# Weight pieces requested one ahead instead of up to four ahead, in an attention + two-MoE kernel

## The chip, the cores and the metric

The kernel runs on one core of a Trainium2 chip. The metric is the device time of one execution in microseconds (us). An execution uses TensorE (PE, and PEld for its weight loads), VectorE (DVE), ScalarE (ACT), GpSimd (POOL), SyncE (SP), which here does nothing but request DMAs, and 16 DMA engines that carry what SP and POOL request.

## What is computed

Three stages follow one another, all in float32:

```python
# 1: block-causal attention, 4 batches x 8 heads x 576 positions x 64
scores = scale * np.matmul(q, k.transpose(0, 1, 3, 2))
mask = block_i >= block_j                      # blocks of 64
attn = softmax(where(mask, scores, -1e9));  x = attn @ v      # as (2304, 512)
# 2: a gated feed-forward layer with d_ff = 1536
gate = 1.0 / (1.0 + np.exp(-(x @ w_gate)));  val = x @ w_val
x = (gate * val @ w_out).astype(np.float32)
# 3: top-1 routing of the 2304 tokens to 8 experts with 1024 hidden columns
out[mask] = gate_w[mask, None] * (np.maximum(xe @ w1[e], 0.0) @ w2[e])
```

The three matrices of stage 2 arrive as 8-byte floats. They have to be turned into pairs of 4-byte numbers (a high and a low part) on the core before TensorE can use them.

## The kernel before, in words

**Attention.** A *pair* is two heads of one batch; there are 16 pairs of five *items* (128 query rows each, the last 64). Pairs 0 to 3, the first batch, run alone ("quick" phase, the function `quick`, up to about 110 us); the other pairs are mixed with stage 2. For a pair `load(p)` requests nine DMAs on SP: keys (two, plus a tail and the tail of the queries into the same tile), queries (two) and values (three). The key tile `k` and the query tile `q` exist once, the value tile `v` twice. So a request for keys waits until the transposes of the keys before have read the tile (L216, the function `prep`), and one for values until the last product with the values of two pairs earlier (L382).

`quick(i)` emits the scores of item i+2 and the product with the values of item i. The load of pair p+1 is written at the end of `quick(i)` for item i = the first of pair p. The transposes of those keys stand in the very next `quick`, which is one item later. The transposed keys are copied by ACT (the tail of the queries, L221, first) and DVE (`kn`, L223), and the scores of the last item of a pair (L256) follow.

**Weights.** Stage 2's matrices are cut into 27 *pieces*, numbered p0, p1, ... here: p0 to p14 have 1024 columns (1 MB each as 8-byte numbers, two DMAs, L557), p15 to p26 have 256. The raw bytes of the large ones go into four tiles (`spare_90` to `spare_93` in the rows, p_n in number n mod 4; p12 to p14 take 91, 92 and 93 again), those of the small ones into three (`wtmp`). A piece is decoded in steps by ACT and DVE: ACT L569 is the first step and the first reader, DVE L574 the last reader of the raw bytes (it frees the tile), then L579, the cast L588 and the subtraction L590. The generator `weights()` emits these steps; `quick` pulls about two steps at each item, so a piece is begun about every second item, and `w_load` requests pieces from inside it. `w_load(NPI)` requests every piece whose tile is free by the order of the program, so up to four ahead.

**Queues.** SP takes its requests in the order in which the program wrote them, and a request that must wait for a tile holds all that come after it. The order on SP is therefore what decides whether keys come before or after weight bytes. PE, ACT, DVE and POOL have orders of their own, given by the program too.

**Stage 2.** Tokens go in units of 256. The attention output x is written to `x_d` by POOL (L393), and `load_x` (L623) reads the four tiles `xu` of a unit back on SP's queue. PE multiplies them with the decoded pieces (`gv`, L634 to L636), ACT and DVE make `g` (L655 to L659), and `acc` (L671) is the product with w_out.

Of the kernel before, what the change touches and what calls it, by code (L numbers as in the profile page):

```python
# [24 lines left out]
def attn_moe_moe_kernel(  # L25
# [473 lines left out]
    NBIG = NW - 3  # L499
    pieces = []  # L500
    for i in range(NW):
        f = i // 3 * 2 + (1 if i % 3 == 2 else 0)
        n = 1024 if i < NBIG else 256
# [11 lines left out]
    NPI = len(pieces)  # L515
# [14 lines left out]
    def before(n):  # L530

        if n >= NBIG:
            return three[n % 3], (n - 3 if n >= NBIG + 3 else -1)
        if n < NW - 6:
            return words[n % 4], n - 4
        return words[(n + 1) % 4], n - 3
# [13 lines left out]
    def w_load(n):  # L550
        while wload[0] < min(n, NPI) and before(wload[0])[1] <= wread[0]:
            dst = before(wload[0])[0]
            o = 0
            for src, r0, nk, c0, ncol in pieces[wload[0]][3]:
                w = nk * ncol * wn
                x = src.bitcast(I32)[r0:r0 + nk * P, c0 * wn:(c0 + ncol) * wn]
                nc.sync.dma_start(  # L557
                    out=dst[:, o:o + w].rearrange("p (k c) -> p k c", k=nk), in_=x.rearrange("(k p) c -> p k c", p=P)
                )
                o += w  # L560
            wload[0] += 1

    def w_round(n, stage):

        raw_ = w_raw(n)
        w0, w1 = raw_[:, :, 0], raw_[:, :, 1]
        b, r = w_buf(n), w_res(n)
        if stage == 0:
            nc.scalar.activation(out=r, in_=w0.bitcast(U32), func=AF.Copy, scale=2.0 ** -29)  # L569
            nc.vector.tensor_scalar(  # L570
                out=b, in0=w1, scalar1=3, scalar2=0x3FFFFFFF, op0=ALU.logical_shift_left, op1=ALU.bitwise_and
            )
        elif stage == 1:
            nc.vector.scalar_tensor_tensor(  # L574
                out=b, in0=w1, scalar=-0x40000000, in1=b, op0=ALU.bitwise_and, op1=ALU.bitwise_or
            )
            wread[0] = n
        else:
            nc.vector.tensor_tensor(out=b, in0=b, in1=r, op=ALU.add)  # L579

    def w_split(n, stage):
        i, c, w, _ = pieces[n]
        while len(wmat) <= i:
            wmat.append(wtile(f"w{len(wmat)}"))
        b = w_buf(n).bitcast(F32)
        h, l = wmat[i][:, c:c + w], wmat[i][:, 1024 + c:1024 + c + w]
        if stage == 0:
            nc.scalar.copy(out=h, in_=b)  # L588
        else:
            nc.vector.tensor_tensor(out=l, in0=b, in1=h, op=ALU.subtract)  # L590
            wdone[0] = n + 1
            if not wide:
                wread[0] = n

    def weights():
        n = 0
        while wdone[0] < NPI:
            if 0 <= n - 2:
                w_split(n - 2, 1)
                yield  # L600
            w_load(NPI)
            if n < NPI and wide:
                w_round(n, 0)
                yield
            if 0 <= n - 1 < NPI and wide:
                w_round(n - 1, 2)
                yield
            if n < NPI and wide:
                w_round(n, 1)
            w_load(NPI)  # L610
            if 0 <= n - 1 < NPI:
                w_split(n - 1, 0)
            n += 1
            yield
# [458 lines left out]
    with tc.manual_schedule():  # L1073
# [3 lines left out]
        def seg():  # L1077
# [3 lines left out]
            return r is not None  # L1081

        wg = weights()
        pace = [0.0]

# [268 lines left out]
```

## Time and profile before

| | us |
|---|---|
| median of 3 runs | 1035.6 |
| the three runs | 1032.04, 1035.6, 1039.47 |
| the profiled execution | 1031.55 |
| its span | 1029.8 |
| PE / DVE / ACT busy in the span | 945.8 / 618.5 / 588.7 |

The span is what the profile covers; the profiled execution's time is 1.75 us more. The busy shares are means over stages with different limits: PE is busy in nine tenths of nearly every slice from about 110 us on, and in five to eight tenths in the first 110 us. The granted clock of TensorE is 0.981 of full on average.

### The profile page before, as it was taken

Reading aid. Unit: us, or ns where it says so; the run is one execution under the profiler, and the core shown is the slowest. Engines: PE = TensorE matmul, PEld = TensorE weight load, DVE = VectorE, ACT = ScalarE, POOL = GpSimd, SP = SyncE. Lnnn points to the kernel's source line nnn. Section 1 sums busy time; section 2 is a strip of 40 time slices with the busy share of each in tenths; the row PEclk is TensorE's granted clock in tenths of the full one; section 3 lists DMA queues with packets and bytes.
Section 4 is the critical chain, followed back from the end, with each engine's and each line's share of the span. In section 5 each row is a group of like instructions: output and inputs, shape, how many; then the busy total and the mean of one; then the engine's idle time right before and its main releaser. Section 6 shows DMA issues by size and latency. Waiting matters only on the chain. (4 is left out here: it accounts for less than half of the span.)

```text
span 1029.8 us, 17756 instructions
## 1 busy us (share of the span) xinstructions
PE 945.8 (92%) x6636; PEld 808.7 (79%) x6636; DVE 618.5 (60%) x1178; ACT 588.7 (57%) x1204; POOL 124.8 (12%) x169
## 2 busy tenths in 40 slices
PE   6557787999999999999999999999989999999994
PEld 3334676888888888988888889999977888888883
DVE  5778886555544544454454421121748999898985
ACT  5667746555555555555555431212248888888884
POOL 1111101110100110010010000000021124122110
PEclk9888999999999999999999999999999999999998
DMA  8853623412132041032040020101352453969110
GB/s 249 255 164 101 174 70 81 127 44 50 41 90 49 17 114 48 22 110 48 17 114 14 17 70 1 62 1 62 133 196 82 167 179 106 359 226 351 47 41 20
DMA packets 111161, 106.07 MB, mean 103 GB/s; under 512 B 62175, under 2 KB 83679, under 8 KB 111072
## 3 DMA queue, kind: packets, MB, share of 16 engines
q1 hardware_dynamic: 104128, 84.97, 27.2%
q0 software_dynamic: 6944, 19.93, 5.8%
q8 instruction: 54, 0.88, 0.4%
q14 instruction: 35, 0.29, 0.1%
HBM read 140.53 MB, written 19.40 MB: 155 GB/s over the span
## 5 line engine op out<-in xcount | busy, mean ns | idle before, releaser
L634 PE MATMUL gv<-xu,w 128*128 128x256 f32 x864 | 254.1, 294 | 3.0 <-DMA xu<-x_d 3.0
L636 PE MATMUL gv<-xu,w 128*128 128x256 f32 x864 | 244.5, 283 | 1.6 <-DVE w L590 1.6
L635 PE MATMUL gv<-xu,w 128*128 128x256 f32 x864 | 244.5, 283 | 0.0
L976 DVE TENSOR_TENSOR el<-raw,eh 128x2048 fp32r<-128x2048 f32 x84 | 191.6, 2288 | 26.9 <-ACT eh L975 25.6
L671 PE MATMUL acc<-w,g 128*128 128x512 f32 x648 | 183.3, 409 | 1.1 <-ACT g L658 1.0
L634 PEld LDWEIGHTS gv<-xu,w 128*128 128x128 f32 x864 | 165.3, 191 | 10.6 <-issue 5.0
L635 PEld LDWEIGHTS gv<-xu,w 128*128 128x128 f32 x864 | 165.6, 192 | 1.4
L636 PEld LDWEIGHTS gv<-xu,w 128*128 128x128 f32 x864 | 165.2, 191 | 1.8 <-DVE w L590 1.8
L975 ACT CAST eh<-raw 128x2048 fp32r<-128x2048 f32 x84 | 161.0, 1917 | 4.4 <-DMA raw<-in_moe_w_dram 4.3
L656 DVE SCALAR_TENSOR_TENSOR th<-th,gv 128x256 f32<-128x256 f32 x108 | 45.3, 420 | 150.7 <-ACT th L655 150.6
L671 PEld LDWEIGHTS acc<-w,g 128*128 128x128 f32 x648 | 110.9, 189 | 21.4 <-issue 3.3
L655 ACT ACTIVATE th<-gv 128x256 f32<-128x256 f32 x108 | 41.6, 385 | 134.0 <-PE gv L636 133.8
L393 POOL DMA_DIRECT2D x_d<-x x80 | 55.0, 688 | 506.1 <-DVE x L391 297.6
L1022 PE MATMUL hp<-eh,xt 128*128 128x512 f32 x320 | 109.1, 402 | 0.0
L1022 PE MATMUL yp<-eh,ht 128*128 128x512 f32 x320 | 106.2, 393 | 0.7 <-ACT ht L1044 0.7
L306 ACT ACTIVATE e<-sp,nm 128x128 f32<-128x128 f32 (+3 forms) x128 | 66.6, 528 | 49.7 <-DVE nm L290 47.0
L658 ACT CAST g<-th 128x256 fp32r<-128x256 f32 x108 | 43.9, 406 | 67.0 <-DVE th L656 62.4
L659 DVE TENSOR_TENSOR g<-th,g 128x256 fp32r<-128x256 f32 x108 | 45.9, 425 | 53.4 <-ACT g L658 53.4
L382 PE MATMUL av<-et,v 128*64 128x128 f32 (+1 forms) x960 | 65.8, 268 | 8.0 <-ACT et L339 7.8
L337 PE MATMUL ep<-ident,e 128*128 128x128 f32 x320 | 58.1, 288 | 13.8 <-DVE e L360 5.6
L1022 PEld LDWEIGHTS yp<-eh,ht 128*128 128x128 f32 x320 | 59.9, 188 | 13.7 <-ACT ht L1044 0.9
L1022 PEld LDWEIGHTS hp<-eh,xt 128*128 128x128 f32 x320 | 60.2, 188 | 11.8
(182 smaller groups left out, 1400.3 us busy)
## 6 DMA issues: line engine op xcount, KB each, us to landing
raw<-in_moe_w_dram SPq DMA_DIRECT2D x88, 1024.0 KB
xu<-x_d SPq DMA_DIRECT2D x36, 256.0 KB
x_d<-x POOLq DMA_DIRECT2D x64, 128.0 KB, 2.2
spare<-in_moe_w_gate_dram SPq DMA_DIRECT2D x10, 512.0 KB
spare<-in_moe_w_val_dram SPq DMA_DIRECT2D x10, 512.0 KB
spare<-in_moe_w_out_dram SPq DMA_DIRECT2D x10, 512.0 KB
x_d<-x2r SPq DMA_DIRECT2D x9, 512.0 KB
k<-in_k_dram SPq DMA_DIRECT2D x32, 128.0 KB
```

The lines of the kernel that those rows point to most:

```text
L306: nc.scalar.activation(out=r["e"][:, j, 0:n], in_=r["view"][:, j, :], func=AF.Exp, bias=r["nm"][:, j:j + 1], accum_out=su[:, j:j + 1],)
L337: nc.tensor.transpose(ep[:, cs], r["e"][:, part, cs], ident)
L382: nc.tensor.matmul(av[hs, 0:m], lhsT=d["v"][:, c, j, :], rhs=rhs, start=(c == 0), stop=(c == t))
L393: nc.gpsimd.dma_start(out=x_d[hp][:, :, t0:t0 + m], in_=x[:, :, 0:m].bitcast(F32))
L634: nc.tensor.matmul(o, lhsT=wh, rhs=x[:, 0, :], start=(kk == 0 and nm == "g"), stop=False, **kw)
L635: nc.tensor.matmul(o, lhsT=wh, rhs=x[:, 1, :], start=False, stop=False, **kw)
L636: nc.tensor.matmul(o, lhsT=wl, rhs=x[:, 0, :], start=False, stop=(kk == KD - 1), **kw)
L659: nc.vector.tensor_tensor(out=g[:, 1, :], in0=th, in1=g[:, 0, :], op=ALU.subtract)
L671: nc.tensor.matmul(o, lhsT=g[:, part, hs], rhs=w_o(w, f), start=(f == 0 and w == "h" and part == 0), stop=(f == KF - 1 and part == 1),)
L975: nc.scalar.copy(out=h, in_=raw[j])
L976: nc.vector.tensor_tensor(out=l, in0=raw[j], in1=h, op=ALU.subtract)
L1022: nc.tensor.matmul(o, lhsT=t[:, cs], rhs=w[:, c * 512:(c + 1) * 512], start=(first and c == 0 and part == 0 and w is eh), stop=(last and c ...
```

## The change

`weights()` counts its rounds with n, and decodes piece n in round n. Before, each round asked `w_load` twice for every piece whose tile is free. Now it asks once, at the round's start, and for a large piece only up to piece n+1; from round 13 on (`NBIG` is 15) for all, as before but once in a round.

```diff
@@ -598,7 +598,7 @@
             if 0 <= n - 2:
                 w_split(n - 2, 1)
                 yield
-            w_load(NPI)
+            w_load(n + 2 if n < NBIG - 2 else NPI)
             if n < NPI and wide:
                 w_round(n, 0)
                 yield
@@ -607,7 +607,6 @@
                 yield
             if n < NPI and wide:
                 w_round(n, 1)
-            w_load(NPI)
             if 0 <= n - 1 < NPI:
                 w_split(n - 1, 0)
             n += 1
```

On PE, DVE, ACT and POOL no instruction moves; SP has the same requests in another order. The first place where they differ is behind p5. Before, SP's order from p5 to the loads of pair 2 is this (`spare_91` is p5, then p6, p7 and p8 in `spare_92`, `spare_93` and `spare_90`; an x2 row is two requests):

```order
L557 DMA spare_91<-in_moe_w_gate_dram 128x4x256
L557 DMA spare_91<-in_moe_w_val_dram 128x4x256
L557 DMA spare_92<-in_moe_w_gate_dram 128x4x256
L557 DMA spare_92<-in_moe_w_val_dram 128x4x256
L557 DMA spare_93<-in_moe_w_out_dram 128x1024 x2
L557 DMA spare_90<-in_moe_w_gate_dram 128x4x256
L557 DMA spare_90<-in_moe_w_val_dram 128x4x256
L186 DMA k<-in_k_dram 128x4x64 x2
L189 DMA k<-in_k_dram 64x2x64
L189 DMA k<-in_q_dram 64x2x64
L186 DMA q<-in_q_dram 128x4x64 x2
```

and with the change, on the same engine from the same p5:

```order
L557 DMA spare_91<-in_moe_w_gate_dram 128x4x256
L557 DMA spare_91<-in_moe_w_val_dram 128x4x256
L186 DMA k<-in_k_dram 128x4x64 x2
L189 DMA k<-in_k_dram 64x2x64
L189 DMA k<-in_q_dram 64x2x64
L186 DMA q<-in_q_dram 128x4x64 x2
L186 DMA v<-in_v_dram 128x4x64 x2
L189 DMA v<-in_v_dram 64x2x64
L557 DMA spare_92<-in_moe_w_gate_dram 128x4x256
L557 DMA spare_92<-in_moe_w_val_dram 128x4x256
L557 DMA spare_93<-in_moe_w_out_dram 128x1024 x2
```

The nine requests of pair 2 have moved ahead of p6, p7 and p8. In the same way those of pair 3 move ahead of p9, p10 and p11, which stood before them, and those of pair 4 ahead of p12 and p13.

The second place is the first `load_x`. Before, SP's order from p13 (`spare_92`) to p14 (`spare_93`) is this:

```order
L557 DMA spare_92<-in_moe_w_out_dram 128x1024 x2
L186 DMA k<-in_k_dram 128x4x64 x2
L189 DMA k<-in_k_dram 64x2x64
L189 DMA k<-in_q_dram 64x2x64
L186 DMA q<-in_q_dram 128x4x64 x2
L186 DMA v<-in_v_dram 128x4x64 x2
L189 DMA v<-in_v_dram 64x2x64
L623 DMA xu<-x_d_57 128x2x256
L623 DMA xu<-x_d_58 128x2x256
L623 DMA xu<-x_d_59 128x2x256
L623 DMA xu<-x_d_60 128x2x256
L557 DMA spare_93<-in_moe_w_gate_dram 128x4x256
```

and with the change, from p12 (`spare_91`) to p14 (the line of `load_x` is now 622):

```order
L557 DMA spare_91<-in_moe_w_gate_dram 128x4x256
L557 DMA spare_91<-in_moe_w_val_dram 128x4x256
L622 DMA xu<-x_d_57 128x2x256
L622 DMA xu<-x_d_58 128x2x256
L622 DMA xu<-x_d_59 128x2x256
L622 DMA xu<-x_d_60 128x2x256
L557 DMA spare_92<-in_moe_w_out_dram 128x1024 x2
L557 DMA spare_93<-in_moe_w_gate_dram 128x4x256
```

The loads of x now stand ahead of p13, and the loads of pair 4 are no longer between them and it. Later one more request changes places: the small piece p24, which stood before the nine loads of pair 5, stands behind them.

## Rows read from the trace of the kernel before

**Rows 1.** The page's first part: busy time of each engine
```profile
PE 945.8 (92%) x6636; PEld 808.7 (79%) x6636; DVE 618.5 (60%) x1178; ACT 588.7 (57%) x1204; POOL 124.8 (12%) x169
```

**Rows 2.** PE's waits, 0 to 220 us: total us, times, longest us
```profile
PE tp L216 <- DMA k<-in_k_dram: 18.7, 3, 7.8
...
PE gv L634 <- DMA xu<-x_d: 3.0, 3, 1.5
```

**Rows 3.** Timeline of PE: start us, us, instruction, count [idle before <- releaser]
```profile
19.10 0.77 PE L216 MATMUL tp<-ident,k 128*128 128x128 f32 x5
...
22.66 1.20 PE L256 MATMUL sp<-kn,qn 64*64 64x512 f32 x8 [1.54 <-DVE kn L223]
...
32.15 0.80 PE L382 MATMUL av<-et,v 128*64 128x64 f32 x20
...
47.98 1.30 PE L216 MATMUL tp<-ident,k 128*128 128x128 f32 x5 [7.78 <-DMA k<-in_k_dram]
...
50.48 2.19 PE L256 MATMUL sp<-kn,qn 64*64 64x512 f32 x8
...
77.28 1.30 PE L216 MATMUL tp<-ident,k 128*128 128x128 f32 x5 [6.71 <-DMA k<-in_k_dram]
...
216.12 0.80 PE L382 MATMUL av<-et,v 128*64 128x64 f32 x20
```

**Rows 4.** Timeline of SP, requests, same columns
```profile
21.13 1.25 SPq L557 DMA_DIRECT2D spare<-in_moe_w_val_dram  x1
28.39 0.37 SPq L557 DMA_DIRECT2D spare<-in_moe_w_gate_dram  x1
...
41.46 0.38 SPq L557 DMA_DIRECT2D spare<-in_moe_w_gate_dram  x1
...
42.49 1.00 SPq L186 DMA_DIRECT2D k<-in_k_dram  x2
...
106.26 2.53 SPq L623 DMA_DIRECT2D xu<-x_d  x4
...
153.64 1.01 SPq L186 DMA_DIRECT2D k<-in_k_dram  x2
...
217.00 0.92 SPq L186 DMA_DIRECT2D v<-in_v_dram  x2
```

**Rows 5.** Timeline of ACT, same columns
```profile
49.31 0.23 ACT L221 ACTIVATE qn<-tp 128x64 f32<-128x64 f32 x1 [6.28 <-PE tp L216]
...
57.82 1.25 ACT L569 ACTIVATE spare<-spare 128x1024 int32<-128x1024 uint32 x1
...
78.62 0.22 ACT L221 ACTIVATE qn<-tp 128x64 f32<-128x64 f32 x1 [6.42 <-PE tp L216]
...
119.42 1.14 ACT L569 ACTIVATE spare<-spare 128x1024 int32<-128x1024 uint32 x1
...
165.92 0.44 ACT L569 ACTIVATE wt<-wtmp 128x256 int32<-128x256 uint32 x1
```

**Rows 6.** Timeline of DVE, same columns
```profile
49.57 0.76 DVE L223 COPY kn<-tp 128x576 f32<-128x576 f32 x1 [6.21 <-ACT qn L221]
...
52.45 0.17 DVE L323 TENSOR_SCALAR su<-su 128x2 f32<-128x2 f32 x1 [1.00 <-ACT e L306]
...
78.88 0.76 DVE L223 COPY kn<-tp 128x576 f32<-128x576 f32 x1 [5.59 <-ACT qn L221]
...
82.00 0.17 DVE L323 TENSOR_SCALAR su<-su 128x2 f32<-128x2 f32 x1 [1.76 <-ACT e L306]
...
119.55 0.42 DVE L659 TENSOR_TENSOR g<-th,g 128x256 fp32r<-128x256 f32 x1 [0.47 <-ACT g L658]
```

**Rows 7.** Stretches: busy us by engine, granted PE clock, DMA share, GB/s
```profile
33.00:34.00 1.00, 0.58 (x4) 0.49 (x6) 1.00 (x4) 0.89 (x1) 0.00 (x0) 1.00 1.13 368
34.00:35.00 1.00, 0.86 (x6) 0.19 (x4) 1.00 (x2) 0.27 (x2) 0.00 (x0) 1.00 0.47 156
...
48.00:53.00 5.00, 5.00 (x25) 3.33 (x27) 2.40 (x5) 3.11 (x8) 0.00 (x0) 0.52 0.53 88
```

## The prediction, made before the change was run

> **What bounds the kernel now.** I began with busy time by engine: PE is busy for 92% of the span, DVE and ACT for under 61% [rows 1]. That mean hides the first 110 us, where the quick attention runs and PE has gaps. So I read PE's waits of the first 220 us. The largest by far is the transposes of the keys waiting for the DMA that brings them: 18.7 us in three waits [rows 2]. One of them is the kernel's very start; the timeline of PE gives the other two, 7.78 us before 47.98 (pair 2) and 6.71 us before 77.28 (pair 3) [rows 3]. Both stop the whole core: in them ACT idles 6.28 and 6.42 us for the transposed tail of the queries [rows 5], and DVE idles 6.21 and 5.59 us behind ACT [rows 6].
>
> Why the keys are late is seen in SP's own timeline. The request for pair 2's keys goes out at 42.49, right behind p8, which goes out at 41.46 [rows 4]. PE had wanted the keys at 47.98 - 7.78 = 40.2, before they were even requested. Their tile was free long before: its last readers, the transposes of pair 1, ended at 19.10 + 0.77 = 19.9 [rows 3]. So the keys waited neither for a tile nor mainly for bandwidth but for their turn on SP, which stood at p6 until 28.39 and at p8 until 41.46 [rows 4] for raw tiles to be freed. Pair 3 repeats this behind p9 to p11.
>
> **The change, part by part.** *Removed:* nothing. PE, DVE, ACT and POOL keep their order, and SP keeps its requests, so all costs lie in when bytes arrive. All times below are those of the old trace ("old time"), minus the gain so far where I say so.
>
> *Keys and queries of pair 2 move ahead of p6 to p8.* The last request before them is now p5, at 21.13 [rows 4], and the tile of keys is free at 19.9. When do they land? p6, requested at 28.39, is the last thing in the DMA engines' backlog before it runs dry between 34 and 35 us (share 1.13, then 0.47) [rows 7]. A piece of 1.05 MB at 368 GB/s takes 2.8 us, so p5 was in by about 34.5 - 2.8 = 31.7. The keys follow it. In the old trace they took 47.98 - 42.49 = 5.5 us with a whole piece ahead of them [rows 3, 4]; that is a generous bound here and gives 37.2, 3 us before 40.2. The first wait goes. For pair 3 the tile is free when pair 2's transposes end (40.2 + 0.77 = 41), with p8 in front; they are in by 48 and are wanted at 77.28 - 6.71 - 6.3 = 64. The second wait goes too.
>
> *What is that worth?* Three engines bound it. DVE's idle time gives 6.21 + 5.59 = **11.8**, since DVE is the fullest engine there; PE's gives 7.78 + 6.71 = **14.5**. Between them lies ACT's, 6.28 + 6.42 = **12.7** [rows 5]. I take ACT's: after each stop DVE's next waits are for ACT's exponentials (1.00 us before 52.45, 1.76 us before 82.00) [rows 6], so ACT, not DVE, says when the work goes on, and PE's larger figure contains time in which ACT and DVE still had old work to do. What is late next is ACT itself, with no wait for a DMA behind it.
>
> *p6 moves behind three value requests.* Those wait until the last product with the values of pair 0 ends, 32.15 + 0.80 = 32.95 [rows 3]; p6 follows at about 35 instead of 28.39. With 5.5 us to land it is in at 40.5; its first decode step is at 57.82 in old time [rows 5], 51.5 after the first gain. Eleven us of cover: nothing. p9 and p12 stand behind the values of pairs 3 and 4 in the same way.
>
> *x moves ahead of p13.* PE waits 3.0 us for the first loads of x [rows 2]; with pair 4's loads gone from in front of them some of that falls away. But the product that follows needs `g`, which DVE delivers at 119.55 + 0.42 = 119.97 [rows 6] at the end of its own and ACT's work; PE would only wait there. I take 0 and keep 3.0 for the range. The price is p13, now requested after x, whose requests end at 106.26 + 2.53 = 108.8 [rows 4]. Landing in 5.5 us it is in at 114.3, five us before its decode at 119.42 [rows 5]; with the slowest landing of this trace, p5's 10.6 us from 21.13 to 31.7, it would just meet it.
>
> *p24 moves behind pair 5's nine requests.* These begin at 153.64 at about half a us each [rows 4], so p24 is at most 5 us later, and in at about 164 against a decode at 165.92 [rows 5]. Nothing, with 2 us to spare.
>
> *TensorE's clock.* After the stop the granted clock is 0.52 from 48 to 53 us, nearly all of it at the 1.2 GHz level [rows 7]. The five transposes take 1.30 us against 0.77 at the full clock, the scores 2.19 against 1.20 [rows 3]: 1.5 us in a stop, 3.0 in two. The Trainium skill (TensorE: Matmul & The Clock Gate, "HAM oscillation — how this bites in real kernels") says that work after a wait for a DMA runs at half clock and counts this as a loss of its own. By it the sum would be 12.7 + 3.0 = 15.7 instead of 12.7. The trace agrees on the clock, but not that this time is on the path here: the waits that follow are DVE's for ACT. I leave it at 0 and carry 3.0 into the range.
>
> **Sum.** 12.7 us off the profiled execution: 1031.55 - 12.7 = 1018.9. That execution lies 4 us under the median of the three runs, 1035.6, and half a us under the fastest of them. I therefore put the gain on the middle of all four, (1032.04 + 1035.6) / 2 = 1033.8, and get **1021**. After the quick phase everything runs in the same order with no deadline of its own, so the gain should reach the end.
>
> **Rivals.**
>
> *A. One stop stays.* "One ahead" holds in the program's order, not in time: SP runs ahead of the other engines, and p2 to p5 stand before pair 2's keys in both orders. If that backlog drains later than I worked out, or the keys' requests wait for something I do not see, the first stop stays and only the second goes: 1033.8 - 6.4 = 1027. For it: only 3 us of cover by the generous bound. Against it: the backlog's end is read off the DMA share. Chance 0.12.
>
> *B. More is won.* The clock stays high and its 3.0 us count, perhaps the 3.0 of x too: 1033.8 - 15.7 = 1018, or 1015 with both. Against it: ACT and DVE end the waits there. Chance 0.10.
>
> *C. Slower: the value requests hold the pieces.* SP now carries the values' wait in front of p6, p9 and p12. Were these tiles released a pair later than I take, 77.28 - 47.98 = 29.3 us, p6 would go out at 62 in old time, 56 after the gain, land at 61.5 and stop ACT from 51.5 on for 10 us; three pieces make 30, and the time 1033.8 - 12.7 + 30 = 1051. It decides from the point where p6 is requested after 51.5 - 5.5 = 46. Against it: a later value request, at 217.00, goes out as soon as its last reader, 216.12 + 0.80 = 216.92, has ended [rows 3, 4]. Chance 0.06. The Trainium skill (DMA: Bandwidth & Descriptors, "Anatomy of one DMA — SWDGE (gpsimd) path") says that waits on semaphores are kept by the issuing sequencer ahead of dispatch and never by the DMA engines; by that rule a held value request does hold the pieces, and p6's held request in this trace agrees.
>
> **Numbers.** My forecast has 0.72. A measurement of this kernel tells about 1%, 10.4 us, from no change. The forecast's 12.7 clears that by 2.3 us, and three runs differ by 7.4, so I count four fifths of it as faster (0.58) and the rest (0.14) as within 1%. B adds 0.10 to faster, A 0.12 to within 1%, C 0.06 to slower: 0.68, 0.26, 0.06. The range runs from B with both its terms, 1015, less 1 for scatter, to A plus 3, 1030; it leaves out C and the tails.
>
> **What would show it.** In the new profile PE's waits for `k` keep only the start's 4.2 us; SP requests pair 2's keys between 22 and 32 us and p6 near 35; ACT's idle time before the tail copies of pairs 2 and 3 falls below 1 us; the first matmul of stage 2 starts 12 to 13 us earlier; and no L569 waits for a DMA. A wait of L569 for p6, p9, p12 or p13, or a `k` wait of several us that stays, would make the forecast wrong, as would a stretch after 110 us that gives the gain back.

## The result: 12.6 us faster, and the profile after

| | us |
|---|---|
| median before, of 4 runs | 1034.57 (1032.04 to 1039.47) |
| median with the change, of 4 runs | 1022.01 (1020.07 to 1022.37) |
| ratio | 0.9869, 95% interval 0.983 to 0.9909 |
| the profiled execution and its span | 1020.07, 1018.3 |

The medians lie 12.56 us apart; forecast were 12.7, and 1021 as the time. The ratio, with its interval, makes the gain 13.6 us (9.4 to 17.6), so the runs alone do not fix it to better than some us. The two profiled executions, 1031.55 and 1020.07, lie 11.48 apart.

PE's waits from 0 to 220 us in the changed kernel come first (total us, times, longest us). They answer to [rows 2]:

```profile
PE tp L216 <- DMA k<-in_k_dram: 3.9, 1, 3.9
PE acc L670 <- ACT g L657: 3.9, 2, 3.1
```

Of three waits for keys, 18.7 us in all, one is left, the kernel's start. The wait for x is gone from the list, and the waits for `g`, 1.0 us before, have grown to 3.9. The first product of stage 2 starts at 97.49 instead of 109.91.

SP's timeline shows why (start us, us, request, count); it answers to [rows 4]:

```profile
20.83 0.82 SPq L557 DMA_DIRECT2D spare<-in_moe_w_val_dram  x1
21.75 3.11 SPq L186 DMA_DIRECT2D k<-in_k_dram  x2
24.90 3.76 SPq L189 DMA_DIRECT2D k<-in_k_dram  x1
...
32.94 0.92 SPq L186 DMA_DIRECT2D v<-in_v_dram  x2
...
34.62 0.53 SPq L557 DMA_DIRECT2D spare<-in_moe_w_gate_dram  x1
...
43.34 0.92 SPq L186 DMA_DIRECT2D k<-in_k_dram  x2
...
82.83 11.77 SPq L622 DMA_DIRECT2D xu<-x_d  x4
94.70 1.01 SPq L557 DMA_DIRECT2D spare<-in_moe_w_out_dram  x2
...
142.86 0.53 SPq L557 DMA_DIRECT2D wtmp<-in_moe_w_gate_dram  x1
```

The keys of pair 2 go out from 21.75 us, right behind p5, instead of from 42.49. The values wait until 32.94 for the last product of pair 0, and p6 follows at 34.62. The keys of pair 3 are requested at 43.34, 21 us before PE uses them.

PE's timeline answers to [rows 3] (start us, us, instruction, count, and in brackets the idle time before it):

```profile
32.07 0.80 PE L382 MATMUL av<-et,v 128*64 128x64 f32 x20
...
41.98 1.33 PE L216 MATMUL tp<-ident,k 128*128 128x128 f32 x5
...
44.41 1.20 PE L256 MATMUL sp<-kn,qn 64*64 64x512 f32 x8
...
64.37 0.82 PE L216 MATMUL tp<-ident,k 128*128 128x128 f32 x5
...
67.56 1.20 PE L256 MATMUL sp<-kn,qn 64*64 64x512 f32 x8 [1.36 <-DVE kn L223]
```

Neither group of key transposes has a bracket: PE comes to them from its own work. ACT's timeline shows the same for the tails of the queries, where [rows 5] had 6.28 and 6.42 us of idle time:

```profile
43.34 0.22 ACT L221 ACTIVATE qn<-tp 128x64 f32<-128x64 f32 x1
...
65.66 0.22 ACT L221 ACTIVATE qn<-tp 128x64 f32<-128x64 f32 x1
...
107.46 1.14 ACT L569 ACTIVATE spare<-spare 128x1024 int32<-128x1024 uint32 x1
...
153.93 0.44 ACT L569 ACTIVATE wt<-wtmp 128x256 int32<-128x256 uint32 x1
```

The last two are the first decode steps of p13 and p24, neither with a wait. DVE's timeline measures the gain at fixed points of the program; the rows answer to [rows 6] one by one:

```profile
43.60 0.76 DVE L223 COPY kn<-tp 128x576 f32<-128x576 f32 x1
...
46.28 0.17 DVE L323 TENSOR_SCALAR su<-su 128x2 f32<-128x2 f32 x1 [0.79 <-ACT e L306]
...
66.76 0.75 DVE L223 COPY kn<-tp 128x576 f32<-128x576 f32 x1
...
69.03 0.17 DVE L323 TENSOR_SCALAR su<-su 128x2 f32<-128x2 f32 x1 [0.69 <-ACT e L306]
...
107.58 0.43 DVE L658 TENSOR_TENSOR g<-th,g 128x256 fp32r<-128x256 f32 x1 [0.47 <-ACT g L657]
```

At the row after the first stop (L323) the program is 52.45 - 46.28 = 6.17 us ahead of before, after the second 82.00 - 69.03 = 12.97, and at the first `g` 119.55 - 107.58 = 11.97. The last gap stays nearly whole to the end of the span, 1029.8 - 1018.3 = 11.5.

### The profile page after: what moved, and what is told of

Read it like the earlier page. It is cut to its first block, busy times and chain, and to the rows that moved or that the text cites. A ratio compares the mean times of both kernels' runs of the same rounds, so it can differ in the third digit from the quotient of the medians.

```text
span 1018.3 us, 17756 instructions
## 1 busy us (share of the span) xinstructions
PE 945.5 (93%) x6636; PEld 809.0 (79%) x6636; DVE 619.3 (61%) x1178; ACT 588.0 (58%) x1204; POOL 122.6 (12%) x169
## 5 line engine op out<-in xcount | busy, mean ns | idle before, releaser
L1021 PEld LDWEIGHTS yp<-eh,ht 128*128 128x128 f32 x320 | 59.9, 188 | 13.6 <-ACT ht L1043 0.9
L1021 PEld LDWEIGHTS hp<-eh,xt 128*128 128x128 f32 x320 | 60.2, 188 | 11.8
```

Of the source, the lines that this page charges most:

```text
L1021: nc.tensor.matmul(o, lhsT=t[:, cs], rhs=w[:, c * 512:(c + 1) * 512], start=(first and c == 0 and part == 0 and w is eh), stop=(last and c ...
```

## Experiments

All ratios are against runs of the kernel before, made beside them (median 1036.24 us for the first four, 1035.18 for the last three). The us behind a ratio are worked out from it and this median.

**Only pair 2's loads moved.** The limit holds in the first five rounds, later all is as before:

```diff
-            w_load(NPI)
+            w_load(n + 2 if n < 5 else NPI)
...
-            w_load(NPI)
+            if n >= 5:
+                w_load(NPI)
```

> Only pair 2's nine loads move ahead of p6 to p8; those of pair 3 stay behind p11 as before. Theory (the gain is two stops of PE, each from the keys' turn on SP, and they add up): the first stop goes, the second stays, 6.2 to 6.4 us less than before, ratio 0.994; PE's waits for keys are 3.9 + 6.7 us. Rival 1 (the keys are late because up to four pieces of weight bytes are in front of them in the DMA engines, so the gain comes from less traffic in the whole phase): p9 to p11 are in flight as before, half the gain or less and a rest of the first stop of several us. Rival 2 (TensorE's clock gives part of it): 1.5 us more, about 8.

Measured: ratio 0.9946 (0.9921 to 0.997), that is 5.6 us (3.1 to 8.2) of 1036.24. The first stop is gone, the second stands; PE's timeline of this kernel:

```profile
42.21 1.12 PE L216 MATMUL tp<-ident,k 128*128 128x128 f32 x5
...
70.91 1.30 PE L216 MATMUL tp<-ident,k 128*128 128x128 f32 x5 [6.06 <-DMA k<-in_k_dram]
```

**Only pair 3's loads moved.** The requests of rounds 5 to 7 are left out, so p9 to p11 come behind pair 3's loads:

```diff
-            w_load(NPI)
+            if not 5 <= n <= 7:
+                w_load(NPI)
```

(at both calls)

> Only pair 3's nine loads move ahead of p9 to p11; pair 2's stay behind p8 as before. Theory: the first stop of 7.8 us stays, the second goes, 6.3 to 6.5 us less than before, ratio 0.994; together with the kernel that moves pair 2 alone it gives the whole gain of the change. Rival 1 (traffic): less than that, and the two alone do not add up to the change. Rival 2 (clock): about 8.

Measured: ratio 0.994 (0.9916 to 0.9964), 6.2 us (3.7 to 8.7). PE's timeline is the mirror image:

```profile
48.47 1.30 PE L216 MATMUL tp<-ident,k 128*128 128x128 f32 x5 [6.89 <-DMA k<-in_k_dram]
...
70.68 1.16 PE L216 MATMUL tp<-ident,k 128*128 128x128 f32 x5
```

The two alone sum to 11.8 us. Each stop goes when its own pair's loads move and stays when only the other's do. The 8 us expected with the clock's part lie inside both intervals, near their upper ends, so these ratios do not settle the clock; the traces do (below).

**Pairs 2 and 3 moved, x and pair 4 not.**

```diff
-            w_load(NPI)
+            w_load(n + 2 if n < 8 else NPI)
...
-            w_load(NPI)
+            if n >= 8:
+                w_load(NPI)
```

> The loads of pairs 2 and 3 move as in the change; from p9 on everything is as before: pair 4's loads stay behind p12 and p13, the first loads of x behind them, p24 ahead of pair 5. Theory (x and pair 4 are worth nothing, PE then waits 3 us for x instead of for g): as fast as the change, 12 to 12.7 us less than before, ratio 0.988. Rival (part of the gain is x, loaded without pair 4 in front): 9 to 10 us less than before.

Measured: ratio 0.9893 (0.9864 to 0.9923), 11.1 us (8.0 to 14.1). The interval takes in both expectations; the trace tells them apart. Here PE still waits for x, though 1.54 us and not the 3 expected, and in the changed kernel it waits for `g` instead. First this kernel's PE:

```profile
100.00 0.39 PE L635 MATMUL gv<-xu,w 128*128 128x256 f32 x1 [1.54 <-DMA xu<-x_d]
```

then the changed kernel's:

```profile
107.61 0.96 PE L670 MATMUL acc<-w,g 128*128 128x512 f32 x3 [3.08 <-ACT g L657]
```

Whether x matters is read from DVE: from its last L323 row of the quick phase to the first `g`. First this kernel,

```profile
93.01 0.17 DVE L323 TENSOR_SCALAR su<-su 128x2 f32<-128x2 f32 x1 [0.69 <-ACT e L306]
...
107.21 0.43 DVE L660 TENSOR_TENSOR g<-th,g 128x256 fp32r<-128x256 f32 x1 [0.47 <-ACT g L659]
```

then the changed one (its `g` at 107.58 is above),

```profile
93.41 0.17 DVE L323 TENSOR_SCALAR su<-su 128x2 f32<-128x2 f32 x1 [0.69 <-ACT e L306]
```

then the kernel before (its `g` at 119.55 is in [rows 6]):

```profile
105.36 0.17 DVE L323 TENSOR_SCALAR su<-su 128x2 f32<-128x2 f32 x1 [0.69 <-ACT e L306]
```

The three stretches take 14.20, 14.17 and 14.19 us. In the one profile of each, moving x brought nothing.

**Keys earlier, pieces as before.** The opposite way to the same place on SP:

```diff
+            if i >= 0 and items[i][1] == 2 and items[i][0] < 2:
+                load(items[i][0] + 2, "kq")
             if i >= 0 and items[i][1] == 0 and 0 < items[i][0]:
-                load(items[i][0] + 1)
+                load(items[i][0] + 1, "v" if items[i][0] < 3 else "kqv")
```

> Weight pieces are requested as before, up to four ahead; instead the keys and queries of pairs 2 and 3 are requested three items earlier in the program, which puts them behind p6 and p9, and only their values stay where they were. Theory (what matters is the keys' place on SP behind a piece that waits for its tile, not how many pieces are ahead): no stop, 12 to 12.7 us less than before, ratio 0.988, keys requested at about 29 us. Rival 1 (pieces in flight): the bytes of p2 to p6 are in front of the keys in the DMA engines, and much of both stops stays: less than half the gain.

Measured: ratio 0.9876 (0.985 to 0.9902), 12.8 us (10.2 to 15.5), with pieces requested up to four ahead; less than half the gain, as rival 1 had it, is excluded. SP's timeline of this kernel (line 559 is `w_load` here):

```profile
30.40 0.37 SPq L559 DMA_DIRECT2D spare<-in_moe_w_gate_dram  x1
30.81 0.51 SPq L559 DMA_DIRECT2D spare<-in_moe_w_val_dram  x1
31.42 1.94 SPq L186 DMA_DIRECT2D k<-in_k_dram  x2
```

The keys stand behind p6 and its bytes and yet are in time: PE's transposes at 42.30 have no wait. So it is not the number of pieces in flight that made them late, but standing on SP behind p8, whose tile is freed last.

**No piece ahead.** The limit is n + 1:

```diff
-            w_load(n + 2 if n < NBIG - 2 else NPI)
+            w_load(n + 1 if n < NBIG - 2 else NPI)
```

> A large piece is requested in the very round that decodes it (limit n + 1 instead of n + 2). Theory (SP runs ahead in time, so the count in the program's order is not a distance in time; p5, p8 and p11 go out behind the values of pairs 2, 3 and 4 at about 35, 57 and 82 us against decodes at 46, 66 and 90 in the change's trace, p12 behind x at about 95 against 99.6): no stop at p5, p8, p11, at most 1.5 us at p12, so 11 to 12.7 us less than before. Rival (one ahead is the least that hides a piece; without it each of ten pieces stops ACT for its landing of some 5 us): slower than before by tens of us.

Measured: ratio 0.9899 (0.9871 to 0.9927), 10.5 us (7.6 to 13.4). The one DMA wait of a decode step is where it was expected, at p12, which now stands behind x, and longer than the 1.5 us allowed. ACT's timeline:

```profile
100.63 1.14 ACT L569 ACTIVATE spare<-spare 128x1024 int32<-128x1024 uint32 x1 [2.56 <-DMA spare<-in_moe_w_val_dram]
```

and SP's, p12 just after the four loads of x:

```profile
80.86 12.25 SPq L622 DMA_DIRECT2D xu<-x_d  x4
93.22 0.54 SPq L557 DMA_DIRECT2D spare<-in_moe_w_gate_dram  x1
```

From request to use it took 7.4 us, more than the 5.5 I had taken from the old trace. It costs about 2.5 us: from DVE's last L323 row of the quick phase to the first `g` it is 16.64 us here (91.92 to 108.56), where the changed kernel has 14.17. "One ahead" is thus not what hides the pieces: with none ahead all but one still come in time, because SP runs ahead of the engines.

**Two and three pieces ahead.** First n + 3 instead of n + 2 in the limit, then only the second call of `w_load` dropped:

```diff
-            w_load(n + 2 if n < NBIG - 2 else NPI)
+            w_load(n + 3 if n < NBIG - 2 else NPI)
```

> Limit n + 3: two pieces ahead. Keys of pair 2 stand behind p6, whose tile is free at 28.3, keys of pair 3 behind p9, free at about 50. Theory (turn on SP): as the change, 12 to 12.7 us less than before. Rival (each piece in flight ahead of the keys costs its share): about two thirds of the gain, 8 us.

Measured: ratio 0.9862 (0.9834 to 0.989), 14.3 us (11.4 to 17.2).

```diff
-            w_load(NPI)          # the second call of a round
```

> Only the second call of w_load in a round is dropped: three pieces ahead. Keys of pair 2 stand behind p7, whose tile is free at 34.6; they go out at about 36 and with the piece in front land at about 41, when PE wants them (40 to 42). Keys of pair 3 stand behind p10, free at about 56 against 64. Theory: a rest of at most 1 us of the first stop, 11 to 12.7 us less than before. Rival (each piece in flight ahead of the keys costs its share): a third of the gain, 4 us.

Measured: ratio 0.9872 (0.9841 to 0.9903), 13.3 us (10.0 to 16.5). SP's timeline of the kernel with three ahead, p7 and then pair 2's keys:

```profile
35.19 0.82 SPq L557 DMA_DIRECT2D spare<-in_moe_w_out_dram  x2
36.10 1.27 SPq L186 DMA_DIRECT2D k<-in_k_dram  x2
```

and PE's:

```profile
42.59 1.12 PE L216 MATMUL tp<-ident,k 128*128 128x128 f32 x5
```

Fourteen us later than in the changed kernel the request is still early enough; no rest of the stop shows. Both intervals exclude the 8 and 4 us of the rivals. The gain is no slope in the number of pieces but a step between the keys behind p7 and the keys behind p8. One, two and three ahead cannot be told apart in time, so none of these kernels beats the change.

## Why the prediction was right, step by step

- **What bounds the phase: right.** The two stops were the loss. Taken one at a time they gave 5.6 and 6.2 us, where ACT's rows said 6.28 and 6.42.
- **Why the keys were late: right.** It was their turn on SP behind a piece that waits for its tile. The diff's count of pieces suggests a queue of bytes; the kernel with early keys and up to four pieces in flight gains as much.
- **The size between its bounds: right, its last us by luck.** The point after both stops moved by 12.97 us, against 11.8 (DVE), 12.7 (ACT) and 14.5 (PE). ACT's idle time comes nearest, and DVE's next rows wait for ACT's exponentials in both traces. But the same point lies 13.8 us ahead in the kernel with no piece ahead (68.18 against 82.00), so ACT's figure is no exact price; the difference is the clock's (below). The medians, with 9.4 to 17.6 us, cannot tell the three figures apart; that they lie within 0.2 us of the forecast is luck.
- **p6 behind the values, p13 behind x, p24 behind pair 5: right.** p6 went out at 34.62 (expected: about 35). No L569 waits for a DMA in the changed kernel's first 200 us. The bound of 5.5 us for a landing was too short as a bound: p12 took 7.4 us where no piece was ahead. p13 had 12.8 us from its request at 94.70 to its decode at 107.46, so a landing of 7.4 would still leave it the five us of cover.
- **x worth nothing: right,** and in the way given: PE's 3.0 us for x became a wait of 3.08 us for `g`, and the first `g` comes no earlier after the quick phase with x early than with x late (14.17 against 14.20 and 14.19 us).
- **The clock: 0 fits the sum, but not for the reason given.** The prediction said that the half clock after a stop is not on the path. In the changed kernel that slow work is gone: the scores behind the stops take 1.20 us each, where they took 2.19 (50.48 in [rows 3], and 79.79). But the granted clock now fell before the first group of transposes, though no DMA stopped PE. The stretches of the changed kernel (us; busy us of PE, PEld, DVE, ACT, POOL; granted clock, DMA share, GB/s):

```profile
36.00:40.00 4.00, 2.91 (x12) 1.57 (x12) 3.63 (x10) 3.17 (x11) 1.16 (x2) 0.65 1.02 300
40.00:44.00 4.00, 4.00 (x22) 2.87 (x21) 3.62 (x7) 2.94 (x8) 0.65 (x3) 0.50 0.89 321
44.00:48.00 4.00, 2.45 (x24) 1.33 (x23) 3.18 (x7) 4.00 (x9) 0.51 (x1) 0.99 1.07 318
```

  From 40 to 44 us that is the half clock (1.2 GHz). In the kernel with early keys, which has the same work on PE, ACT and DVE, the clock is 1.00 in all three stretches. What that is worth is read between two of DVE's L323 rows, the one ahead of the first stop and the one behind it. Ahead of it, in the kernel before (the row behind is 52.45 in [rows 6]),

```profile
31.59 0.17 DVE L323 TENSOR_SCALAR su<-su 128x2 f32<-128x2 f32 x1 [0.28 <-ACT e L306]
```

  in the changed kernel (behind it: 46.28, above),

```profile
31.50 0.17 DVE L323 TENSOR_SCALAR su<-su 128x2 f32<-128x2 f32 x1 [0.28 <-ACT e L306]
```

  and both rows with early keys:

```profile
33.60 0.17 DVE L323 TENSOR_SCALAR su<-su 128x2 f32<-128x2 f32 x1 [0.28 <-ACT e L306]
...
47.42 0.17 DVE L323 TENSOR_SCALAR su<-su 128x2 f32<-128x2 f32 x1 [0.23 <-ACT e L306]
```

  The stretch takes 20.86, 14.78 and 13.82 us. At the full clock the first stop is thus worth 7.04 us, about half way from ACT's 6.28 to the 7.8 that the clock's 1.5 would make of it; the changed kernel got 6.08. It lost the 0.96 us where ACT waits for PE. The first such row, in the changed kernel,

```profile
38.43 0.37 ACT L339 COPY et<-ep 128x256 f32<-128x256 f32 x1 [0.83 <-PE ep L337]
```

  and with early keys:

```profile
40.29 0.37 ACT L339 COPY et<-ep 128x256 f32<-128x256 f32 x1 [0.57 <-PE ep L337]
```

  Slow rows of PE that nobody waited for cost nothing here: with pair 2's loads alone moved, the scores ahead of the transposes took 1.79 us and the transposes 1.12 (1.13 and 0.77 with early keys), and the stretch took 13.80 us all the same. So part of the clock's time was on the path; the sum came out near 12.7 because the half clock, in its new place, took about what its end behind the stops gave. That is luck. The effect lies inside the 3.0 us that the range carried.

- **Rival C did not come:** the values were requested at 32.94, 0.07 us after their tile's last reader, 32.07 + 0.80. PE's list does name the values once, 1.70 us before 83.18; but the same product waits 1.67 us in the kernel before too (95.24, there for ACT), so this is no new loss.
- **What I had not forecast:** the lead falls by 1 us from 12.97 at 69.03 to 11.97 at the first `g`, and by another 0.5 to the end. In the changed kernel the clock falls once more around 76 us. PE's row there, a product that takes 1.09 us at the full clock in the trace of before, and after it ACT's row, which waits for it:

```profile
75.19 1.97 PE L382 MATMUL av<-et,v 128*64 128x128 f32 x14 [0.50 <-ACT et L339]
```

```profile
77.20 0.27 ACT L390 CAST x<-av 128x128 fp32r<-128x128 f32 x1 [2.06 <-PE av L382]
```

  The same row of the kernel before:

```profile
89.29 0.27 ACT L390 CAST x<-av 128x128 fp32r<-128x128 f32 x1 [1.18 <-PE av L382]
```

  That is 0.9 us on the path at this place, again where PE is what ACT waits for; it was a loss, not the gain of rival B. Why the clock fell there stays open, as does the last 0.5 us. Both are within what runs differ by.

## What to carry to other kernels

On a queue that issues in order, look at what each request stands behind and when that one may go, not at how many requests are ahead: a small urgent load behind a prefetch that waits for its buffer waits for the buffer too. Either side can be moved, the urgent load earlier or the prefetch later; it is enough that the last request ahead of it is one whose buffer is free in time. When a stop halts several engines, price it by the idle time of the engine that the next waits name, to within what TensorE's clock moves (here up to 1 us at a stop, and only where another engine waits for PE), and check that what becomes early, here x, is not simply waited for elsewhere.

## What the runs showed of the hardware that I had not expected

- **The requests for keys right behind p5 took long.** Between 20 and 30 us of the changed kernel the DMA share is full, and the requests that took about half a us each at 43.34 (0.92 for two) took up to 3.76:

```profile
20.00:30.00 10.00, 6.33 (x62) 4.57 (x61) 9.52 (x16) 10.00 (x21) 1.57 (x3) 1.00 1.07 378
```

  So SP itself was held for 7 us in the keys' first three requests, which the prediction had not looked for; it was harmless here. A full DMA share alone does not explain it: in the kernel before the share is 1.07 over the same 10 us too, and p6's request at 28.39 took 0.37 us [rows 4]. What held the keys' requests stays open.
- **The granted clock differs between executions of one kernel.** The six executions of the kernel with two pieces ahead had mean granted clocks from 0.974 to 0.987. The profiled one had the lowest and took 1028.65 us, where their median is 1021.69; the changed kernel's profiled one took 1020.07 at 0.986. A comparison of these two profiles alone would have called two pieces ahead 8.6 us slower, while the medians call it equal.
